# Linear attention and SwiGLU on one core: earlier start of the inputs, two more units turned by VectorE, weights' sums and two states moved

One Trainium2 chip (trn2), one core. The metric is the device time of one execution in microseconds (us). Most executions of one kernel agree within 0.3%.

## The reference

```python
# attention: B, H, S, D = 4, 8, 768, 48
for t in range(S):
    cur = einsum('bhd,bhe->bhde', u * k[t], v[t])
    y[t] = einsum('bhd,bhde->bhe', r[t], state + cur)
    state = w * state + einsum('bhd,bhe->bhde', k[t], v[t])
# x = y as (B*S, H*D) = (3072, 384); d_ff = 1536
g = x @ w_gate
out = (g * sigmoid(g) * (x @ w_val)) @ w_out
```

## The kernel before

A unit is 128 time steps of one batch (24 in all). For each, GpSimd scales k and r by powers of w, both are transposed, TensorE makes scores, outputs (y) and the state's update (u), and gates and projections of the feed-forward part fill TensorE between them. Units below `BLOCKS` are transposed by TensorE. Later ones are moved in 32-row blocks by 16 DMAs and then transposed by VectorE. Cuts are marked with `...`.

```python
for t in v_ld:
    dve.memset(t[:, :, D:64], 0.0)
dve.memset(hats[:, 0:6, :, D:64], 0.0)
dve.memset(wcol[:], 1.0)
for z in Z:
    pool.memset(z[:], 0.0)
for e in range(2):
    sp.dma_start(out=wcol[64 * e : 64 * e + D, :], in_=w...)
load(0)                         # k, r of unit 0, also by sp
...
make_identity(nc, ident[:])
warm(18)                        # dummy matmuls: TensorE's clock
...
dve.tensor_scalar(held[:], wcol[:], W_LOW, W_HIGH, ALU.max, ALU.min)
for l in range(7):              # L280: powers of w by doubling
    dve.tensor_mul(pw[:, :, P - 2 * n : P - n], pw[:, :, P - n : P], f)
...
own_product(0)                  # GpSimd: r * k, then * u

def rhat_of(i):
    return rhat[i % 2 if i < BLOCKS else i % 4 // 2]

def move_blocks(i):             # L356
    first, step = ((0, 1), (11, -1), (12, 1), (23, -1))[i % 4]
    for m in range(4):
        for q in range(4):
            sp.dma_start(out=..., in_=...)      # 32 x 256 values

def turn_blocks(i):             # L371
    for dst, src in ((kT[i % 2], blocks[0]), (turned[i], blocks[1])):
        dve.transpose(dst, src)

def weight_sum():               # L476, four times, 128 x 1152
    pool.tensor_sub(o, a, b)
...
turn(3)
dve.tensor_copy(w128[:].unsqueeze(2), pw[:, :, 0:1])
scores(2)
...
outputs(2)
load(4)
round_act()
feed(1)
outputs(3)
scale_k(3)
round_act()
round_pool()
scale(4)
load_v(4)
feed(1)
update(2)
update(3)
...
BLOCKS = 12
for s in range(4, N + 2):
    if 4 < s < N: own_sum(s)
    if s + 1 < N:
        scale(s + 1); own_product(s + 1); load_v(s + 1); load(s + 3)
    if s < BLOCKS: turn(s)
    gaps(s, 0)
    ... scores(s - 1) ...
    if BLOCKS <= s < N: turn_blocks(s)
    if BLOCKS <= s + 1 < N: move_blocks(s + 1)
    ...
```

Of the kernel before, what the change touches and what calls it, by code (L numbers as in the profile page):

```python
# [15 lines left out]
P = 128  # L16
# [6 lines left out]
def fast(  # L23
# [25 lines left out]
    B, H, S, D = r.shape  # L49
# [5 lines left out]
    N = B * NCH  # L55
    DM, DFF = moe_w_gate.shape
# [11 lines left out]
    dve, pool, act, pe, sp = nc.vector, nc.gpsimd, nc.scalar, nc.tensor, nc.sync  # L68


    wcol = cst.tile([P, HP], FP32, name="wcol")
# [3 lines left out]
    w128 = cst.tile([P, HP], FP32, name="w128")  # L75
# [11 lines left out]
    Z = [cst.tile([P, HP, D2], FP32, name=f"Z{b}") for b in range(B)]  # L87
# [12 lines left out]
    blocks = [hats[:, n].rearrange("p h x -> p (h x)") for n in (7, 6)]  # L100

    def rhat_of(i):
        return rhat[i % 2 if i < BLOCKS else i % 4 // 2]

    def raw(i):

# [125 lines left out]
    def own_sum(i):  # L232
        dus[i] = three.tile([P, H], FP32, name="du", tag="du")
        dve.tensor_reduce(dus[i][:], rks.pop(i), axis=AX.X, op=ALU.add)


    sg0 = two.tile([P, 1], FP32, name="sg0", tag="sg0")
    for t in v_ld:
        dve.memset(t[:, :, D:64], 0.0)
    dve.memset(hats[:, 0:6, :, D:64], 0.0)  # L240
    dve.memset(wcol[:], 1.0)
    for z in Z:
        pool.memset(z[:], 0.0)
    for e in range(2):
        sp.dma_start(out=wcol[64 * e : 64 * e + D, :], in_=w.rearrange("(a e) d -> e d a", e=2)[e])
    load(0)
    sp.dma_start(
        out=ub[:].rearrange("p h d -> p (h d)"),
# [10 lines left out]
    def warm(n):  # L259

        ps = ps_a.tile([P, HP, P], FP32, name="warm", tag="a")
        for _ in range(n):
            pe.matmul(ps[:, 0, :], ident[:], ident[:], start=True, stop=True)

    warm(18)

    pool.memset(mask[:], 1.0)
    pool.affine_select(
        out=mask[:], in_=mask[:], compare_op=ALU.is_gt, fill=0.0,
        base=0, pattern=[[1, P]], channel_multiplier=-1,  # L270
    )
    dve.tensor_scalar(held[:], wcol[:], W_LOW, W_HIGH, ALU.max, ALU.min)
    tables = two.tile([P, 2, HP, P + 32], FP32, name="tables", tag="hT")
    pw, pv = tables[:, 0, :, 0 : P + 1], tables[:, 1, :, 0:P]
# [2 lines left out]
    for l in range(7):  # L277
        n = 1 << l
# [19 lines left out]
    def scale_k(i):  # L298
        pool.tensor_mul(khat[i % 4][:, :, 0:D], raw(i)[0], kscale[:])  # L299
# [15 lines left out]
    def diagonal(i):  # L315

        du = dus.pop(i)
        on_act = HP if i < 4 else H
        small.extend(
            lambda h=h: act.activation(  # L320
                At[i % 2][:, h, :], ident[:], AF.Identity, scale=du[:, h : h + 1]
            )
            for h in range(on_act)
        )
        if on_act < H:
            n = H - on_act
            pool.tensor_mul(
                At[i % 2][:, on_act:H], ident[:].unsqueeze(1).to_broadcast([P, n, P]),
                du[:, on_act:H].unsqueeze(2).to_broadcast([P, n, P]),
            )  # L330
# [58 lines left out]
    def outputs(i):  # L389



        c, b = divmod(i, B)
        A, vl, z = At[i % 2], v_ld[i % 4], Z[b]
        rT = turned.pop(i)
        ps = ps_a.tile([P, CC, P], FP32, name="y_ps", tag="a")
        cols = [[] for _ in range(4)]
        for m in range(4 * CC):
            (cc, q), (a, s) = divmod(m, 4), divmod(m, 3)
            each = [(z[0:R2, a, 32 * s : 32 * s + 32], rT[0:R2, at(i, a), :])] if c > 0 else []  # L400
            if s < 2:
                each.append((vl[:, a, 32 * s : 32 * s + 32], A[:, 2 * a, :]))
            if s > 0:
                each.append((vl[:, a, 32 * s + 16 : 32 * s + 48], A[:, 2 * a + 1, :]))
            cols[q] += [(cc, x, n == 0, n == len(each) - 1) for n, x in enumerate(each)]
        for n in range(len(cols[0])):
            for q in range(4):
                cc, x, start, stop = cols[q][n]
                pe.matmul(  # L409
                    ps[32 * q : 32 * q + 32, cc, :], *x,  # L410
                    start=start, stop=stop, skip_group_check=True,
                )
        act.copy(xT[:, i % NX, :, :], ps[:])  # L413
# [57 lines left out]
    def weight_sum():  # L471

        n = len(summed)
        o = (wt[1][:], w12, wt[0][:], wt[2][:])[n]
        a, b = ((w22, w12), (w12, w11), (w22, w12), (w21, wt[0][:]))[n]
        pool.tensor_sub(o, a, b)  # L476
        summed.append(n)

    part_of = {}
# [18 lines left out]
    def project(g, n):  # L498

        h11, h12, h21, h22 = h_quarters(g)  # L500
        x = part_of.setdefault(g, {})
        if n == 0:
            one_bank = ps_f.tile([P, 2, 2 * P], FP32, name="o_f", tag="gv")[:, 0, 0:NH]
            if g % 2 == 0:
                x["a"] = ps_o.tile([P, 2 * P], FP32, name="o_a", tag="o")[:, 0:NH]
                x["b"] = one_bank
            else:
                x["a"] = one_bank
                x["b"] = ps_w.tile([P, 2 * P], FP32, name="o_b", tag="w_mag")[:, 0:NH]
            x["out"] = [two.tile([P, DM], FP32, name=n, tag=n) for n in ("o_sb1", "o_sb2")]  # L510
        lhs, rhs, acc = (
            (h11, w11, "a"), (h12, w21, "b"), (1, wt[0], "a"), (2, wt[1], "a"),
            (0, w12, "b"), (h22, wt[2], "a"), (3, w22, "b"),
        )[n]
        if isinstance(lhs, int):
            lhs = x["s"][lhs]
        ps = x[acc]
        for f in range(FH):
            pe.matmul(  # L519
                ps, lhs[:, f, :], rhs[:, f, :],  # L520
                start=(f == 0 and n in (0, 1, 4)), stop=(f == FH - 1), skip_group_check=True,
            )
        o1, o2 = x["out"]
        if n in (0, 2, 3):
            nm = {0: "p1", 2: "u2", 3: "u3"}[n]
            x[nm] = six.tile([P, 2 * P], FP32, name=nm, tag="part")[:, 0:NH]
            act.copy(x[nm], ps)
        elif n == 1:
            dve.tensor_add(o1[:, 0:NH], x["p1"], ps)
        elif n == 5:  # L530
            act.copy(o2[:, 0:NH], ps)
        elif n == 6:
            dve.tensor_add(o1[:, NH:DM], x["u2"], ps)  # L533
        if n in (3, 4):
            if "c22" in x:
                dve.tensor_add(o2[:, NH:DM], x["u3"], x["b"])
            x["c22"] = True
        if n >= 5:
            j = 6 - n
            c, b = divmod(2 * g + j, B)  # L540
            n0 = S * b + P * c
            act.dma_start(out=out[n0 : n0 + P, :], in_=x["out"][j][:])



# [130 lines left out]
    def feed(n, pops=1):  # L676
        for _ in range(n):
            ready = [k for k, (need, _) in enumerate(todo) if need <= done["pool"] + len(summed)]
            if ready:
                todo.pop(ready[0])[1]()  # L680
            for _ in range(min(pops, len(small))):
                small.popleft()()
# [32 lines left out]
                feed(1, 3)  # L715

    share = [0]
    BLOCKS = 12
    LATE = 12
    EARLY = {s: ("" if s < 7 else "R", "F", "R", "F", "RF") for s in range(5, 12)}  # L720
    EARLY[4] = ("R", "F", "", "F", "F")
# [6 lines left out]
    turn(0)  # L728
    natural_tables()
    own_sum(0)  # L730
    diagonal(0)
    flush()
    own_product(1)
# [38 lines left out]
    flush()  # L772
    own_product(3)
    turn(3)
    dve.tensor_copy(w128[:].unsqueeze(2), pw[:, :, 0:1])
    scores(2)
    update(0)
    update(1)
# [6 lines left out]
    load(4)  # L785
    round_act()
    feed(1)
    outputs(3)
    scale_k(3)
    round_act()  # L790
    round_pool()
    scale(4)
    load_v(4)
    feed(1)
    update(2)
    update(3)
    round_pool()
    own_product(4)
    load(5)
# [4 lines left out]
    for s in range(4, N + 2):  # L804
        if 4 < s < N:
            own_sum(s)
        if s + 1 < N:
            scale(s + 1)
            own_product(s + 1)
            load_v(s + 1)  # L810
            if s + 3 < N:
                load(s + 3)
        if s < BLOCKS:
            turn(s)
        gaps(s, 0)
        if 4 <= s - 1 < N:
            while small:
                small.popleft()()
            scores(s - 1)
            if s >= LATE:  # L820
                outputs(s - 2)
                update(s - 2)
            gaps(s, 1)
        if BLOCKS <= s < N:
            turn_blocks(s)
        if BLOCKS <= s + 1 < N:
            move_blocks(s + 1)
        gaps(s, 2)
        if s - 2 >= 4 and (s < LATE or s > N):
            outputs(s - 2)  # L830
            update(s - 2)
        if s >= 5 and s % 2:
            queue((s - 3) // 2)
        if s < N:
            diagonal(s)
        if s - 2 >= 4:
            gaps(s, 3)
        gaps(s, 4)
        if s == 12:

            dve.tensor_tensor(bad[:], held[:], wcol[:], ALU.not_equal)
            dve.tensor_reduce(badc[:], bad[:], axis=AX.X, op=ALU.add)
            dve.memset(ones[:], 1.0)
            n_ps = ps_a.tile([P, HP, P], FP32, name="n_ps", tag="a")
            pe.matmul(n_ps[0:1, 0, 0:1], badc[:], ones[:], start=True, stop=True)
            act.copy(outside, n_ps[0:1, 0, 0:1])
# [417 lines left out]
```

## Time and profile before

| | before |
|---|---|
| time, median of 3 | 625.08 us (624.19 to 625.53) |
| span in the profile | 623.3 us |
| TensorE busy | 98% |
| u of unit 4 begins | 59.33 us |
| u of unit 10 begins | 133.76 us |

TensorE bounds the kernel after about 58 us; the prediction shows the lines. I use two marks that can be read in every trace: the start of u (the state's update on TensorE) of unit 4 tells what the beginning is worth. The stretch from there to u of unit 10, 74.43 us here, tells what the stages around units 10 and 11 are worth. One place in that stretch matters below: the first pair's second and third projections. TensorE's timeline before (start, length, engine, line, operation, out<-in, shapes, count):

```profile
125.16 4.07 PE L519 MATMUL o_f<-wo,hT 128*128 128x192 f32 x24
```

The second and third projections run as one group of 24 matmuls, with no wait.

### The profile page before, as it was taken

What the parts mean: (1) busy time and instruction counts of PE and PEld (TensorE: products, weight loads), DVE (VectorE), ACT (ScalarE), POOL (GpSimd) and SP (SyncE); (2) the same over time, 40 slices, a digit from 0 to 9 for tenths busy, and PEclk for the clock granted to TensorE, in tenths of its full rate; (3) what the DMA queues carried; (4) which work ended last, traced back from release to release, by engine and by line L of the source; (5) the groups of instructions that cost most, each with busy time, mean ns of one, the idle gap of its engine ahead of it and who ended that gap; (6) DMA issues with size and microseconds to landing.
All of it is one profiled execution on the core that took longest, in us unless ns stands there. A gap on an engine that the chain in (4) does not pass through costs nothing.

```text
span 623.3 us, 13014 instructions
## 1 busy us (share of the span) xinstructions
PE 611.0 (98%) x5040; PEld 552.1 (89%) x5040; DVE 358.6 (58%) x751; ACT 238.9 (38%) x647; POOL 296.9 (48%) x350
## 2 busy tenths in 40 slices
PE   8799999999999999999999999999999999999996
PEld 7688888899888899888899888899988899988896
DVE  6888997373566574466575355574354463355460
ACT  3368785312444412344331335422243321233310
POOL 4789789935556315364452636341334211443110
PEclk9999999999999999999999999999999999999999
DMA  7989873233232213322223312221000000000001
GB/s 187 218 215 252 260 242 65 50 62 82 57 60 34 40 16 76 65 42 46 44 34 70 78 16 32 31 41 38 26 1 2 2 0 26 26 1 2 1 2 56
DMA packets 138008, 40.47 MB, mean 65 GB/s; under 512 B 128592, under 2 KB 131792, under 8 KB 137936
## 3 DMA queue, kind: packets, MB, share of 16 engines
q1 hardware_dynamic: 134480, 34.82, 26.4%
q10 hardware_dynamic: 3456, 4.72, 2.1%
q8 instruction: 42, 0.69, 0.5%
q14 instruction: 30, 0.25, 0.1%
HBM read 28.51 MB, written 4.72 MB: 53 GB/s over the span
## 4 chain that ended last, share of the span: by engine, by line
PE 90%; POOL 2%; DMA 1%; ACT 1%; DVE 1%; issue 0%; SPq 0%; ACTq 0%; POOLq 0%
PE c_b L625 25%; PE c_a L625 21%; PE o_f L519 13%; PE o_a L519 8%; PE gv L448 7%; PE o_b L519 6%; PE y_ps L409 5%; PE s_ps L379 3%; PE u_ps L424 1%; PE tp L341 1%; DMA r_ld<-in_r_dram 1%; POOL wg L216 1%; POOL wv L216 1%; POOL rk L228 0%; POOL hats L299 0%
## 5 line engine op out<-in xcount | busy, mean ns | idle before, releaser
L609 POOL TENSOR_TENSOR hT<-hT,u 128x256 f32<-128x256 f32 x60 | 47.0, 785 | 148.7 <-DVE hT L608 121.6
L632 ACT COPY u<-c_a 128x256 f32<-128x256 f32 x120 | 44.5, 371 | 85.8 <-PE c_a L625 83.3
L625 PE MATMUL c_a<-t,wv 128*128 128x256 f32 x240 | 72.1, 382 | 0.1
L625 PE MATMUL c_b<-xT,wg 128*128 128x256 f32 x240 | 71.7, 380 | 0.0
L605 ACT ACTIVATE sg<-hT 128x256 f32<-128x256 f32 x120 | 50.0, 416 | 52.5 <-DVE hT L634 33.8
L320 ACT ACTIVATE At<-ident,du 128x128 f32<-128x128 f32 x176 | 62.0, 398 | 16.0 <-DVE o_sb L533 7.2
L625 PE MATMUL c_b<-xT,s 128*128 128x256 f32 x240 | 61.7, 380 | 0.0
L639 DVE TENSOR_TENSOR u<-u,c_b 128x256 f32<-128x256 f32 x60 | 25.1, 419 | 60.5 <-PE c_b L625 55.4
L625 PEld LDWEIGHTS c_a<-t,wv 128*128 128x128 f32 x240 | 45.0, 190 | 6.8 <-ACT u L632 1.2
L625 PEld LDWEIGHTS c_b<-xT,s 128*128 128x128 f32 x240 | 45.3, 190 | 6.5
L625 PEld LDWEIGHTS c_b<-xT,wg 128*128 128x128 f32 x240 | 45.4, 190 | 5.9
L634 DVE TENSOR_TENSOR hT<-p,c_b 128x256 f32<-128x256 f32 x60 | 25.2, 420 | 41.7 <-PE c_b L625 39.1
L585 POOL TENSOR_TENSOR s<-wv,wg 128x256 f32<-128x256 f32 x24 | 17.6, 734 | 65.5 <-PE o_f L519 50.8
L384 DVE COPY_PREDICATED At<-mask,s_ps 128x512 f32<-128x512 int32 x48 | 33.0, 741 | 21.3 <-PE s_ps L379 12.4
L302 POOL TENSOR_TENSOR hats<-r_ld,rscale 128x384 f32<-128x384 f32 x20 | 20.8, 1040 | 35.3 <-DMA hats<-hats 25.2
L448 PE MATMUL gv<-xT,wg 128*128 128x256 f32 x144 | 36.7, 391 | 0.6 <-ACT xT L413 0.6
L637 DVE TENSOR_TENSOR hT<-hT,c_a 128x256 f32<-128x256 f32 x60 | 25.3, 421 | 19.5 <-PE c_a L625 18.3
L641 DVE TENSOR_TENSOR hT<-u,c_b 128x256 f32<-128x256 f32 x60 | 25.2, 421 | 19.4 <-PE c_b L625 19.2
L625 PE MATMUL c_b<-t,s 128*128 128x256 f32 x120 | 36.2, 383 | 0.0
L409 PE MATMUL y_ps<-At,v_ld 128*32 128x128 f32 x768 | 34.9, 273 | 1.3 <-DVE At L384 1.3
L625 PE MATMUL c_b<-xT,wv 128*128 128x256 f32 x120 | 35.9, 381 | 0.0
L625 PE MATMUL c_a<-t,s 128*128 128x256 f32 x120 | 35.8, 380 | 0.0
(135 smaller groups left out, 1384.3 us busy)
## 6 DMA issues: line engine op xcount, KB each, us to landing
hats<-hats SPq DMA_DIRECT2D x192, 32.0 KB, 2.0
w_bits<-in_moe_w_gate_dram SPq DMA_DIRECT2D x6, 768.0 KB, 6.4
v_ld<-in_v_dram SPq DMA_DIRECT2D x48, 96.0 KB, 3.3
w_bits<-in_moe_w_val_dram SPq DMA_DIRECT2D x6, 768.0 KB, 6.3
w_bits<-in_moe_w_out_dram SPq DMA_DIRECT2D x6, 768.0 KB, 6.7
out_dram<-o_sb ACTq DMA_DIRECT2D x24, 192.0 KB, 1.9
k_ld<-in_k_dram SPq DMA_DIRECT2D x20, 192.0 KB, 3.1
r_ld<-in_r_dram SPq DMA_DIRECT2D x20, 192.0 KB, 3.8
```

Of the source, the lines that this page charges most:

```text
L320: lambda h=h: act.activation(At[i % 2][:, h, :], ident[:], AF.Identity, scale=du[:, h : h + 1])
L384: dve.copy_predicated(At[i % 2][:].rearrange("p (a e) t -> p a e t", e=2)[:, :, e], mask[:].bitcast(INT32).unsqueeze(1).to_broadcast([P, H ...
L409: pe.matmul(ps[32 * q : 32 * q + 32, cc, :], *x, start=start, stop=stop, skip_group_check=True,)
L448: pe.matmul(gv[:, o, :].rearrange("p (i t) -> p i t", i=2), wt[:, c, P * f : P * (f + 1)], xT[:, 2 * g % NX : 2 * g % NX + 2, c, :], start ...
L519: pe.matmul(ps, lhs[:, f, :], rhs[:, f, :], start=(f == 0 and n in (0, 1, 4)), stop=(f == FH - 1), skip_group_check=True,)
L605: act.activation(x[what, f][:], h[j], AF.Sigmoid)
L609: pool.tensor_mul(h[1], h[1], x.pop(("u3", f))[:])
L625: pe.matmul(ps.rearrange("p (i t) -> p i t", i=2), lhs, rhs, start=first, stop=what not in ("p2", "p5", "p4", "p3"), skip_group_check=True,)
L632: act.copy(x[nm, f][:], ps)
L634: dve.tensor_add(h[0], x.pop(("p1", f))[:], ps)
L637: dve.tensor_mul(h[0], h[0], ps)
L641: dve.tensor_add(h[1], x.pop(("u2", f))[:], ps)
```

## The change

It has six parts. A: the memset of w's column comes first and w goes by ScalarE's queue, so that SyncE begins with k; 11 instead of 18 warm multiplies; the Z memsets behind the mask. B: units 10 and 11 turned by VectorE, and `turn` ahead of the scaling in the loop. C: the weights' sums on VectorE. D: the states of units 2 and 3 right behind y of unit 3. E: the w128 copy early. F: the last output stored in two halves. The intent is an earlier start and less work on TensorE.

```diff
-        return rhat[i % 2 if i < BLOCKS else i % 4 // 2]
+        return rhat[i % 2 if i < 8 else i % 4 // 2]
@@
+    dve.memset(wcol[:], 1.0)
     for t in v_ld:
         dve.memset(t[:, :, D:64], 0.0)
     dve.memset(hats[:, 0:6, :, D:64], 0.0)
-    dve.memset(wcol[:], 1.0)
-    for z in Z:
-        pool.memset(z[:], 0.0)
     for e in range(2):
-        sp.dma_start(out=wcol[64 * e : 64 * e + D, :], in_=w...)
+        act.dma_start(out=wcol[64 * e : 64 * e + D, :], in_=w...)
@@
-    warm(18)
+    warm(11)
     ... (mask) ...
+    for z in Z:
+        pool.memset(z[:], 0.0)
@@ weight_sum
-        pool.tensor_sub(o, a, b)
+        dve.tensor_sub(o, a, b)
@@ (part F, the last output in two halves: cut)
-    BLOCKS = 12
+    BLOCKS = 10
@@
     own_sum(0)
+    dve.tensor_copy(w128[:].unsqueeze(2), pw[:, :, 0:1])
@@
-    dve.tensor_copy(w128[:].unsqueeze(2), pw[:, :, 0:1])
     scores(2)
@@
+    scale_k(3)
     outputs(3)
-    scale_k(3)
+    update(2)
+    update(3)
     round_act()
     ...
     feed(1)
-    update(2)
-    update(3)
@@ loop over s
+        if s < BLOCKS:
+            turn(s)
         if s + 1 < N:
             scale(s + 1) ...
-        if s < BLOCKS:
-            turn(s)
```

More of the change, by code (lines that the diff above doesn't have):

```diff
@@ L240, in fast @@
     dve.memset(hats[:, 0:6, :, D:64], 0.0)
-    dve.memset(wcol[:], 1.0)
-    for z in Z:
-        pool.memset(z[:], 0.0)
     for e in range(2):
-        sp.dma_start(out=wcol[64 * e : 64 * e + D, :], in_=w.rearrange("(a e) d -> e d a", e=2)[e])
+        act.dma_start(out=wcol[64 * e : 64 * e + D, :], in_=w.rearrange("(a e) d -> e d a", e=2)[e])
     load(0)
@@ L537, in project, with store @@
             x["c22"] = True
-        if n >= 5:
-            j = 6 - n
+        def store(j, cols):
             c, b = divmod(2 * g + j, B)
             n0 = S * b + P * c
-            act.dma_start(out=out[n0 : n0 + P, :], in_=x["out"][j][:])
+            act.dma_start(out=out[n0 : n0 + P, cols], in_=x["out"][j][:, cols])
+        ends = g == N // 2 - 1
+        if n == 1 and ends:
+            store(0, slice(0, NH))
+        elif n >= 5:
+            store(6 - n, slice(NH if n == 6 and ends else 0, DM))
     PLACE = {
```

## The prediction

> **What bounds the kernel now.** I read the page's shares first, then the slices, the chain that ended last, the timelines of the first 60 us and of 100 to 136 us, and the groups by form.
>
> ```profile
> span 623.3 us, 13014 instructions
> PE 611.0 (98%) x5040; PEld 552.1 (89%) x5040; DVE 358.6 (58%) x751; ACT 238.9 (38%) x647; POOL 296.9 (48%) x350
> ...
> PE   8799999999999999999999999999999999999996
> ...
> POOL 4789789935556315364452636341334211443110
> ...
> PE 90%; POOL 2%; DMA 1%; ACT 1%; DVE 1%; issue 0%; SPq 0%; ACTq 0%; POOLq 0%
> ```
>
> TensorE bounds the kernel. Only the first two slices (0 to 31 us) and the last are not full, and GpSimd (POOL) is full in the third to eighth slices. In the chain in order of time everything from 57.8 us to the end is TensorE; before that it runs through POOL:
>
> ```profile
> 52.90 1.80 POOL wv L216
> 54.73 0.93 ACT w_low L179
> 57.76 1.75 PE y_ps L409 x56
> 59.85 5.38 PE gv L448 x24
> ```
>
> So a gain before 57.8 us counts if it moves that POOL chain; after it, only TensorE work removed or a new TensorE wait counts. The start, from the timeline:
>
> ```profile
> 0.80 1.48 POOL L243 MEMSET Z<- 128x384 f32 x4 [0.29 <-POOLq L1248]
> 2.08 0.88 SPq L245 DMA_DIRECT2D wcol<-in_w_dram  x2
> 2.84 6.83 PE L263 MATMUL warm<-ident 128*128 128x128 f32 x36 [2.84 <-POOL ident masks.py:199]
> 3.00 0.45 SPq L115 DMA_DIRECT2D hats<-in_k_dram  x1
> 4.53 0.17 DVE L272 TENSOR_SCALAR held<-wcol 128x4 f32<-128x4 f32 x1 [2.49 <-DMA wcol<-in_w_dram]
> 7.52 0.99 POOL L228 TENSOR_TENSOR rk<-hats 128x384 f32<-128x384 f32 x1 [4.22 <-DMA hats<-in_r_dram]
> 9.39 0.91 PEld L341 LDWEIGHTS tp<-ident,hats 128*128 128x128 f32 x8
> 26.61 0.96 DVE L775 COPY w<-tables 128x4 f32<-128x4 f32 x1
> ```
>
> k and r are there by 7.5 us, but the first real transpose starts at 9.39: the warm matmuls hold TensorE until then, and the tables made from w end at 9.06 (7.63 + 1.43, same view).
>
> **What the Trainium skill says.** (1) "TensorE: Matmul & The Clock Gate", "What's actually happening": the array runs at half clock until a free-running window of about 3.4 us was busy. The trace agrees: the warm weight loads take 334 ns until about 7.3 us and 192 ns from 8.5. (2) "SBUF — State Buffer", "Who interferes with whom": a VectorE op of the two-port kind or with two SBUF inputs and a GpSimd op block each other whole. The 128x4 copy of L775 took 0.96 us beside a GpSimd multiply of 1.01 us that had begun at 26.54. (3) "DMA: Bandwidth & Descriptors", "Anatomy of one DMA": about 2 us fixed per DMA; the page here has 2.0 us for the hats<-hats moves. It reads them as fixed latency; issue is what I must add to it below.
>
> **The change, part by part.**
>
> *Start.* SyncE no longer waits for the memset of wcol nor issues w: k goes out at about 0.8 instead of 3.00, and the whole input stream behind it moves up by 2.2 us (the first eight slices are DMA-heavy, so it stays shifted). w goes out by ScalarE's queue at about 1.0 instead of 2.08 and lands at about 3.5 to 4.0 instead of 4.5: tables end at 8.0 to 8.6. ident is ready 1.4 us earlier, as the Z memsets move behind; 11 warm multiplies at two passes of about 0.213 us (cold start-to-start) run 1.4 to 6.1. Then the transposes run as soon as k and r land (about 5.3) and VectorE's first table multiply starts at about 8.1 to 8.6 instead of 10.14. That is 1.5 to 2.2, say 2.0 us, up to 20 us. Seven fewer warm multiplies alone are worth nothing beyond this, as they lie beside the wait for the tables.
>
> *w128.* VectorE has no listed wait from 20.57 to 30.8 us, so the 0.96 us there come off: gain 2.9 at 31 us. At its new place VectorE had 0.67 us idle.
>
> *States of 2 and 3.* Their four VectorE multiplies (1.47 us at 39.54) now come ahead of the second chunk's rounding, which ended at 38.34. POOL wanted that chunk at 39.30, so about 1.47 - 0.96 = 0.5 us are lost on the POOL chain. TensorE fills a 0.60 us wait with the u products, but is held by POOL there anyway. Gain at 57.8 us: 2.9 - 0.5 = 2.4 us.
>
> *Units 10 and 11.* 16 transposes leave TensorE. By the chain eight take 0.87 us, with the step to the scores 0.97: 1.94 us on a full TensorE. Four ScalarE copies (0.58 each) go, four VectorE transposes (0.71 + 0.67 per unit) come, and 32 moves of 32 KB. Those are the dear part:
>
> ```profile
> 118.82 0.37 SPq L115 DMA_DIRECT2D k_ld<-in_k_dram  x1
> 119.87 10.90 SPq L356 DMA_DIRECT2D hats<-hats  x16
> 132.57 1.02 POOL L302 TENSOR_TENSOR hats<-r_ld,rscale 128x384 f32<-128x384 f32 x1 [7.98 <-DMA hats<-hats]
> 123.83 0.42 DVE L455 TENSOR_TENSOR sg<-sg,gv 128x256 f32<-128x256 f32 x1 [2.41 <-ACT sg L454]
> ```
>
> Sixteen issues take 10.9 us, and GpSimd's next rhat waits 1.8 us past them. A stage here lasts only 12.15 us (tp at 101.67 and 113.81). In the times of the kernel before: the k load for unit 12 is issued at 94.14, so unit 10's moves run 95.2 to 106.0; rhat of 11, which overwrites their source, starts at 107.8; then the k product to 109.9, the load of unit 13 to 111.0, unit 11's moves to 121.9, landed about 123.6. VectorE meets unit 11's transposes at about 118.3 in its order, so it sits about 5 us, then has 1.38 (transposes), 0.74 (Z) and 0.85 (the last gate's two multiplies) before it: done at about 126.6. Those multiplies free the PSUM bank for the second projection, which TensorE began at 125.16 and would now reach at 125.16 - 1.94 = 123.2. So it waits 3.4 us, and the pair nets 126.6 - 125.1 = 1.5 us worse instead of 1.94 better. Unit 12 and later have stages twice as long and are not held.
>
> *Weights' sums.* Four GpSimd ops of 2.65 us become VectorE ops of about 1.3 (0.95 for 768 columns, times 1152/768, minus a fixed part). GpSimd has room for them, VectorE too, beside the wait above; GpSimd needs the relief, as it now waits at rhat of 11. Nothing on TensorE's path.
>
> *End.* The last store carries half the bytes; landing is mostly fixed (1.9 us): 0.2 us.
>
> Sum: -2.4 + 1.5 - 0.2 = -1.1, about 624.0; without the wait at unit 11: -2.4 - 1.94 - 0.2 = -4.5, about 620.5.
>
> **Rivals.** (a) The moves hide. For it: VectorE does only 58% overall, and if issue is faster with less traffic, or unit 10's moves begin earlier, each us saved in one set of moves comes off twice. Against: both sets measured 10.9 and 10.5 us. It gives 620.5. (b) My main account, 624.0: the transfer's latency takes the place of the transposes removed. (c) The start gives less: w from ScalarE shares the rings with k and r and lands no earlier, or TensorE goes cold between 6 and 8 us; gain 1 instead of 2.4, hence 622 to 625.4 with (a) or (b). (d) The start gives more: POOL keeps all of the 2.9 and the half us is not lost; 620.0 with (a), 623.5 with (b).
>
> **Range and chances.** I put 0.55 on the wait at unit 11 costing most of what I worked out, and 0.45 on it being small. The mean of 624.0 and 620.5 with these weights is 622.4; I say 622.5, with 619.5 to 624.9 for 8 in 10. The 2% border is at 612.6 and 637.6: no sum of the parts comes near either, so within 2% has 0.97.
>
> **What would show it.** Right: first transposes at about 6 to 7 us; VectorE's first table multiply before 8.7; the w128 copy away from 26 us; TensorE's steady stretch begins about 2.4 us earlier, as does y of unit 4 (57.76 before); VectorE idle for 3 to 5 us at unit 11's kT transposes, released by hats<-hats, and TensorE idle up to 3.4 us before the second projection's o_f. If neither idle stretch is there, (a) is right. Wrong altogether: a TensorE wait after 140 us, new waits of GpSimd at the w sums, or a first TensorE wait that grew for lack of k and r.

## The result, and the profile after

The changed kernel takes 628.4 us, median of 6 (627.33 to 631.55), against 625.12 us (624.19 to 625.53) of the kernel before. The ratio is 1.0064, 95% interval 1.0037 to 1.009. Ratios are the mean time of one kernel's fast runs over that of the other's of the same rounds, so not quite the ratio of the medians quoted. The result is within 2%, but it lies outside my range and on the other side of the kernel before. All runs count as fast, yet they spread over 4 us, with mean granted clocks of 0.99 to 1.0.

The page of the profile after, span and busy times:

```profile
span 627.2 us, 12991 instructions
PE 608.4 (97%) x5010; PEld 547.2 (87%) x5010; DVE 368.2 (59%) x759; ACT 236.9 (38%) x643; POOL 290.2 (46%) x346
```

TensorE does 2.6 us less work (611.0 before), and the span is 3.9 us longer: all of the loss, and more, is waiting. The two marks are 59.50 us for u of unit 4 (59.33 before) and 78.12 us for the stretch to unit 10 (74.43 before). From there to the end nothing more is lost: 3.86 us of the 3.93 us by which the last projection ends later are there at unit 10.

**The start.** Timeline after, all engines:

```profile
5.31 0.17 DVE L272 TENSOR_SCALAR held<-wcol 128x4 f32<-128x4 f32 x1 [3.25 <-DMA wcol<-in_w_dram]
5.54 1.01 POOL L228 TENSOR_TENSOR rk<-hats 128x384 f32<-128x384 f32 x1 [2.23 <-DMA hats<-in_r_dram]
5.72 3.22 DVE L280 TENSOR_TENSOR tables<-tables 128x4 f32<-128x4 f32 x7
8.99 0.66 PE L308 MATMUL t_ps<-ident,tables 128*128 128x128 f32 x4 [2.08 <-DVE tables L280]
10.38 0.68 DVE L343 TENSOR_TENSOR kT<-tp,tables 128x512 f32<-128x512 f32 x1
```

k and r land 2 us earlier (GpSimd's product begins at 5.54, 7.52 before), but w lands later, 5.31 against 4.53. The list of DMA issues shows it; its last column is the median time from issue to landing, of the kernel before and then of the one after:

```profile
wcol<-in_w_dram SPq DMA_DIRECT2D x2, 0.8 KB, 1.9
```

```profile
wcol<-in_w_dram ACTq DMA_DIRECT2D x2, 0.8 KB, 3.3
```

On ScalarE's queue w travels beside k and r, and takes 3.3 us instead of 1.9; its own queue did not bring it earlier here. Then the seven doublings took 3.22 us, against 1.85 before, because GpSimd's products now lie beside them. Part of that is won back: before, the last multiply of the tables (L284, at 7.63) lay beside GpSimd's product and took 1.43 us, after only 0.69. So the tables end 5.15 us after w, 4.53 before, and with the later w they end at 10.46 instead of 9.06. The first table multiply starts at 10.38, not at 8.1 to 8.6. That is only 0.24 us later than before (10.14), because before it had waited for TensorE's transposes, which began at 9.39. TensorE, which had run out of warm multiplies, stands idle for 2.08 us. GpSimd's first addition of low parts (L197), where its long chain begins, starts at 18.00 us, against 18.01 before: of the 2.0 us that the start was to give up to 20 us, nothing is there.

**The states.** VectorE and GpSimd after:

```profile
35.64 1.45 DVE L434 TENSOR_TENSOR Z<-u_ps,w 48x192 f32<-48x192 f32 x4
37.13 0.56 DVE L188 TENSOR_SCALAR wv<-w_mag 128x384 int32<-128x384 int32 x1
39.48 1.83 POOL L216 TENSOR_TENSOR wv<-wv,w_low 128x768 int32<-128x768 int32 x1 [0.64 <-DVE wv L189]
```

The Z multiplies of units 2 and 3 stand between the roundings of two chunks, and GpSimd, whose chain sets the pace up to unit 4, waits 0.64 us for the second.

**Units 10 and 11.** The queue of SyncE, GpSimd, VectorE and TensorE after:

```profile
97.10 11.90 SPq L356 DMA_DIRECT2D hats<-hats  x16
111.40 1.01 POOL L302 TENSOR_TENSOR hats<-r_ld,rscale 128x384 f32<-128x384 f32 x1 [5.67 <-DMA v_ld<-in_v_dram]
114.48 11.23 SPq L356 DMA_DIRECT2D hats<-hats  x16
127.11 0.71 DVE L371 STREAM_TRANSPOSE kT<-hats 128x512 f32<-128x512 f32 x1 [4.34 <-DMA hats<-hats]
```

```profile
130.09 2.19 PE L519 MATMUL o_f<-wo,hT 128*128 128x192 f32 x12 [2.27 <-DVE hT L456]
132.84 1.38 PE L519 MATMUL o_a<-wt,hs 128*128 128x192 f32 x7 [0.56 <-DVE hs L493]
```

The chain of the prediction is there: moves of 10, scaled r of 11, moves of 11, VectorE waiting 4.34 us, TensorE waiting 2.27 us. But it is the third projection that waits, not the second. In this one trace two more things came on top, which the later trace of the same kernel (run 16) does not show: a chunk of weights landed late (the stretch up to unit 7 was 0.98 us longer), and a gate waited 1.10 us at 116 us.

### The profile page after: what moved, and what is told of

Same layout as the page of the kernel before. It is cut to its first block, busy times and chain, and to the rows that moved or that the text cites. A ratio compares the mean times of both kernels' runs of the same rounds, so it can differ in the third digit from the quotient of the medians.

```text
span 627.2 us, 12991 instructions
## 1 busy us (share of the span) xinstructions
PE 608.4 (97%) x5010; PEld 547.2 (87%) x5010; DVE 368.2 (59%) x759; ACT 236.9 (38%) x643; POOL 290.2 (46%) x346
## 4 chain that ended last, share of the span: by engine, by line
PE 78%; DVE 4%; POOL 4%; SPq 3%; DMA 2%; ACT 2%; issue 1%; ACTq 0%; POOLq 0%; DVEq 0%
PE c_b L630 25%; PE c_a L630 21%; PE o_f L519 12%; PE o_a L519 7%; PE o_b L519 6%; PE y_ps L409 4%; SPq L356 3%; PE s_ps L379 2%; DMA w_bits<-in_moe_w_out_dram 1%; ACT At L320 1%; POOL rk L228 1%; DMA r_ld<-in_r_dram 1%; POOL wo L216 1%; POOL wg L216 1%; ACT w_low L179 1%
```

## The experiments

Sixteen kernels ran, one of them the changed kernel again. The kernel before was timed in each job: median 625.10 (runs 1 to 4), 625.02 (5 to 8), 625.47 (9 to 12), 625.69 (13 to 16). "Stretch" is from u of unit 4 to u of unit 10 in the profiled execution.

| run | time, median (range) | ratio, 95% interval | u of unit 4 | stretch |
|---|---|---|---|---|
| before | | | 59.33 | 74.43 |
| changed | 628.4 (627.33-631.55) | 1.0064, 1.0037-1.0090 | 59.50 | 78.12 |
| 1 not units | 627.47 (625.67-628.90) | 1.0046, 1.0033-1.0059 | 59.53 | 74.43 |
| 2 units only | 625.98 (625.00-628.01) | 1.0021, 1.0005-1.0036 | 58.94 | 74.25 |
| 3 start only | 625.49 (624.54-626.77) | 1.0005, 0.9992-1.0018 | 59.80 | 74.43 |
| 4 w128, states | 625.89 (625.64-626.46) | 1.0014, 1.0001-1.0027 | 59.89 | 74.43 |
| 5 sums on GpSimd | 628.37 (627.47-629.32) | 1.0055, 1.0041-1.0068 | 59.63 | 76.50 |
| 6 start, 18 warms | 624.54 (624.02-625.57) | 0.9997, 0.9983-1.0010 | 58.28 | 74.51 |
| 7 GpSimd held | 624.98 (623.99-625.39) | 0.9999, 0.9985-1.0012 | 58.12 | 74.43 |
| 8 w first | 623.67 (623.32-624.52) | 0.9981, 0.9967-0.9994 | 57.82 | 74.43 |
| 9 filled, 16 | 627.53 (627.11-629.49) | 1.0034, 1.0021-1.0047 | 61.55 | 76.26 |
| 10 unit 11 only | 625.19 (624.52-626.97) | 0.9996, 0.9982-1.0009 | 59.24 | 73.55 |
| 11 alternate buffers | 626.38 (625.07-626.73) | 1.0011, 0.9998-1.0024 | 58.76 | 74.62 |
| 12 filled, sums on GpSimd | 627.72 (627.26-629.27) | 1.0043, 1.0030-1.0056 | 59.75 | 76.25 |
| 13 states on start | 625.36 (624.97-626.88) | 1.0000, 0.9988-1.0012 | 59.53 | 74.43 |
| 14 w first, unit 11 | 623.82 (623.13-624.44) | 0.9976, 0.9963-0.9989 | 58.28 | 73.55 |
| 15 filled, 9 | 627.72 (627.29-628.60) | 1.0036, 1.0023-1.0049 | 61.47 | 75.12 |
| 16 changed again | 628.44 (626.41-629.91) | 1.0039, 1.0023-1.0055 | 61.54 | 76.83 |

The marks are single traces; where they and the times differ, I say so.

**1. All parts but B.**

```diff
 # the changed kernel, with BLOCKS = 12, turn(s) behind the scaling, rhat_of as before
```

> All of the change except that units 10 and 11 stay with TensorE. Theory W (the chain of 32 moves at units 10 and 11 cost TensorE about 4.4 us between 102 and 133 us, set against 1.94 us saved): about 2 to 2.5 us under the changed kernel in the same job, that is 625.5 to 626.5, with no TensorE wait longer than 0.6 us between 100 and 140 us and no VectorE wait for hats<-hats there. Rival S (the loss comes from the start and the order of rounding, the moves net to nothing): same time as the changed kernel, 628.

Measured 627.47 us, with one execution at 625.67 (clock 1.0) and two near 628.8 (clock 0.992). The stretch is that of the kernel before, so B accounts for the whole lengthening of the stretch. The median lies between the two expectations (625.5 to 626.5, and 628), so neither theory had the time right. The parts outside B gain nothing at unit 4, and the slow executions are those with a low clock.

**2. B alone on the kernel before.**

```diff
-    BLOCKS = 12
+    BLOCKS = 10
 # turn(s) ahead of scale(s + 1); rhat_of with i < 8
```

> The kernel before with only the units 10 and 11 moved to VectorE (with the order of turning and scaling that it needs), weights' sums still on GpSimd. Theory W: slower than before by 1.5 to 4 us, a VectorE wait of 3 to 5 us at unit 11's kT transposes released by hats<-hats; GpSimd's sums (4 x 2.65 us) may delay unit 11's scaling further. Rival S: within 0.5 us of before or up to 1.9 us faster.

```profile
122.86 0.71 DVE L371 STREAM_TRANSPOSE kT<-hats 128x512 f32<-128x512 f32 x1 [5.09 <-DMA hats<-hats]
```

```profile
125.84 2.19 PE L519 MATMUL o_f<-wo,hT 128*128 128x192 f32 x12 [0.70 <-POOL wt L476]
128.42 2.19 PE L519 MATMUL o_a<-wt,hs 128*128 128x192 f32 x12 [0.39 <-DVE hs L493]
```

The first fence is VectorE, the second TensorE. VectorE waits 5.09 us at 122.86, as predicted ("about 5 us"), and TensorE waits 0.70 and 0.39 us at the third and fourth projections. The stretch is 0.18 us shorter, not 1.5 us longer: the bank that the late gate frees is used by the third projection, one projection (1.95 us from start to start) later than I had it. Where the 1.94 us go can be read: up to u of unit 9 the stretch is 1.74 us shorter (58.99 us, 60.73 before), and the last stage, from there to u of unit 10, is 1.56 us longer (15.26, 13.70 before). In time this kernel is none the less slower than the kernel before by 0.2% (1.0005 to 1.0036), 0.9 us in the medians, which is neither theory W's 1.5 to 4 us nor rival S's 0.5 us at most. Half of the executions were nevertheless at 626.75 to 628.01 us, at clocks of 0.995 to 0.998, and the other half at 625.0 to 625.2.

**3. A alone.**

```diff
 # kernel before, with w by act, wcol memset first, Z memsets behind the mask, warm(11)
```

> The kernel before with only the new start: w by ScalarE's queue, SyncE begins with k, 11 warm multiplies, memsets reordered. From the trace of the changed kernel (first transposes at 5.8 us, but tables multiplied only from 10.38 against 10.14) I expect no gain: 624.6 to 625.6, the w column landing at about 5.3 us against 4.5, and the seven doubling multiplies of the tables taking about 3.2 us against 1.85 because GpSimd's rk products run beside them. The prediction's theory would have it 2 us faster.

Windows of this trace (stretch, length, busy time and count of PE, PEld, DVE, ACT, POOL, then the granted clock, the DMA share, GB/s):

```profile
8.00:12.00 4.00, 1.93 (x10) 1.73 (x11) 3.83 (x10) 0.63 (x2) 0.00 (x0) 0.78 1.08 334
12.00:16.00 4.00, 4.00 (x43) 3.79 (x42) 2.02 (x4) 2.81 (x7) 3.02 (x3) 0.80 1.38 222
```

TensorE is busy for only 1.93 of 4 us in 8 to 12 us, and its clock falls to 0.78 and 0.80. u of unit 4 comes at 59.80, later than before. Three executions had a clock of 0.995 and took 626.2 to 626.8 us; three had 0.998 to 1.0 and took 624.5 to 624.8. So the shorter warm-up is no mere saving.

**4. D and E alone.**

```diff
 # kernel before, with the w128 copy behind own_sum(0), and scale_k(3), outputs(3), update(2), update(3)
```

> The kernel before with only the two small moves: the w128 copy early, the states of 2 and 3 right behind y of 3. If the 0.96 us of the copy come off VectorE's stretch and the states' 1.45 us ahead of the second rounding take them back, as the trace of the changed kernel suggests (wv rounding at 37.13 against 36.14, GpSimd's wv add at 39.48 against 39.30): within 0.4 us of before. If the prediction's sizes were right: 0.4 to 0.5 us faster.

u of unit 4 came 0.56 us later than before, and the time was 625.89 us. My prediction gave these two parts 0.4 us of gain (0.96 minus 0.5). The w128 copy took 0.16 us at its new place, but VectorE then waited 0.49 us for scores at 26.96, so only half of the 0.96 us arrived: VectorE's next masked copy is 0.53 us ahead of the kernel before (26.96, 27.49), and the one after that only 0.15 us (31.84, 31.99). The states then took 0.7 us. The expectation (within 0.4 us of before) failed: the median is 0.79 us above.

What takes away the second part of the gain shows in all traces. With the copy at its new place VectorE waits 1.57 to 1.58 us for the masked copy of unit 3 (at 31 to 33.5 us; nine traces: the changed kernel, runs 1, 4, 5, 9, 12, 14, 15 and 16). With the copy at the old place it waits 1.22 us in all nine others. So the early copy itself comes with 0.36 us lost at that step; why, no run shows.

**5. The sums back on GpSimd.**

```diff
-        dve.tensor_sub(o, a, b)
+        pool.tensor_sub(o, a, b)
```

> The changed kernel with the four weights' sums back on GpSimd. Theory P (the sums on VectorE cost: 1.6 to 2.1 us each instead of the 1.3 I had estimated, GpSimd's rk products beside them twice as long, both ahead of unit 11's moves and of the last gates): 1.5 to 2.5 us under the changed kernel, 626 to 627, and VectorE at unit 11's kT transposes by about 123 instead of 127.1 us. Rival: the sums are neutral and 628 stays.

628.37 us, ratio 1.0055: not told apart from the changed kernel, which was not in this job (1.0064 in its own, 1.0039 in run 16). TensorE's wait at the third projection was 1.90 us here, and behind it the clock fell to 0.81 (125 to 130 us) and 0.85 (130 to 135 us): the twelve matmuls took 3.83 us instead of 2.11. The sums are not what costs, though on VectorE they took 1.64 to 2.13 us each, not the 1.3 us I had worked out.

**6. A with the 18 warm multiplies kept.**

```diff
-    warm(11)
+    warm(18)
```

> The new start alone, but with all 18 warm multiplies. Theory C (the idle stretch of TensorE between the first transposes and the tables lets its clock fall in some executions, which is why the start alone ran at 624.5 to 624.8 with a mean clock of 0.998 and at 626.2 to 626.8 with 0.995): every execution at 624.5 to 625.5 and no mean clock of 0.995 or less. Rival D (the two levels come from the transfers): two levels again.

Three executions took 624.02 to 624.54 us at a clock of 0.999, two 625.52 and 625.57 at 0.996. The group of run 3 at 0.995 and over 626 us is gone, as theory C has it; a smaller second group remains. u of unit 4 is at 58.28: this start is worth 1.05 us there, not 2.4. The time is not told apart from the kernel before (0.9983 to 1.0010).

**7. GpSimd held until the tables are done.**

```diff
+    junk = cst.tile([P, 1], FP32, name="junk")
+    pool.tensor_copy(junk[:], pv[:, 0, 0:1])     # waits for the tables
     own_product(0)
```

> As the run before it, and GpSimd held until the tables are made by a one-column copy from them. Theory P (two VectorE inputs in SBUF against a GpSimd op): the seven doublings take 1.85 us again instead of 3.2, the tables are done about 1.3 us earlier (9.8 instead of 10.4), and as rk of unit 0 then starts late, at most 0.5 us come off the total. Rival: the doublings stay at 3.2 us because of something else.

```profile
5.63 1.85 DVE L280 TENSOR_TENSOR tables<-tables 128x4 f32<-128x4 f32 x7
```

With GpSimd out of the way the doublings take 1.85 us again, as before the change. That shows the cause of the 3.22 us. It gains little at unit 4 (58.12), as GpSimd's product then comes late.

**8. w by SyncE, ahead of k.**

```diff
-        act.dma_start(out=wcol...
+        sp.dma_start(out=wcol...
```

> As the run before it, but w goes out by SyncE ahead of k again, right after the early memset of wcol. If k and r ahead of w on the shared rings are what made w land at 5.3 instead of 4.5 us: w lands at 3.3 to 3.6, the tables are done by 8.2, the first table multiply at 8.2 to 8.9 instead of 10.14, and the whole is 0.5 to 1.5 us under the kernel before. If the landing of w does not follow the order of issue: no change against the run before it.

```profile
3.41 0.17 DVE L272 TENSOR_SCALAR held<-wcol 128x4 f32<-128x4 f32 x1 [1.35 <-DMA wcol<-in_w_dram]
```

This kernel also keeps run 7's holding of GpSimd. w lands at 3.41, and the tables are done at 7.19 instead of 10.46. 623.67 us, faster than the kernel before (ratio at most 0.9994), and u of unit 4 is 1.51 us earlier. So w behind k and r was the wrong thing to change: w is 0.8 KB and the tables wait for it. The edit moves w back to SyncE's queue and ahead of k at once, so the runs do not tell which of the two did it.

**9. The changed kernel with TensorE's idle times filled.**

```diff
-    warm(11)
+    warm(18)
@@ ahead of the third projection of the first pair
+            if g == 0 and (j, p) == (0, 1):
+                warm(16)
```

> The changed kernel with 18 warm multiplies at the start again and 16 more dummy multiplies (about 1.7 us at full clock) put on TensorE just ahead of the third projection of the first pair, where it stood idle for 2.27 us. My theory: part of the loss is the clock that falls behind such an idle stretch (0.80 behind the start with 11 warms, 0.81 behind the projection's wait in an earlier trace). Then no slice of the trace but the first shows a clock under 1.0, the executions lie within 1 us of each other at clocks of 0.996 or more, and the time is 626 to 627 instead of 628.4. Rival, waits alone: the executions still spread over 627 to 631 us with clocks of 0.993 and the median stays near 628.

The dummies took about 3.5 us, not 1.7, and so overshot the wait by about 2 us (the last gate ended at 129.16, the projection began at 131.15). At the projections the clock stays at 1.00. But the profiled execution (629.49 us) shows a fall at another place:

```profile
25.00:26.00 1.00, 0.32 (x9) 0.13 (x5) 1.00 (x3) 0.57 (x2) 1.00 (x2) 1.00 1.08 348
...
29.00:30.00 1.00, 1.00 (x10) 0.90 (x8) 0.95 (x3) 0.00 (x0) 0.00 (x0) 0.50 0.76 283
...
33.00:34.00 1.00, 1.00 (x4) 0.82 (x3) 0.90 (x2) 1.00 (x3) 0.16 (x1) 0.50 0.07 16
```

From 28 to 34.5 us TensorE runs at half clock, though no wait of it in the 8 us before was longer than 0.69 us; u of unit 4 comes at 61.55. My expectation (all executions within 1 us, clocks of 0.996 or more) failed.

**10. Only unit 11 turned by VectorE.**

```diff
-    BLOCKS = 12
+    BLOCKS = 11
 # on the kernel before, with the rest of part B
```

> The kernel before with only unit 11 turned by VectorE. Eight transposes leave TensorE (0.97 us with the step to the scores), and only one set of moves comes ahead of unit 12's. If the loss of the pair is that two sets of about 11.3 us follow each other in stages of 12, then unit 11's moves start near 96 to 107 us, VectorE's kT transpose of unit 11 waits for no DMA for more than 0.5 us, u of unit 10 begins at about 132.8 instead of 133.76, and the time is 624.0 to 624.4. Rival, that the place of the turn ahead of the scaling or VectorE's transposes themselves cost it: u of unit 10 at 133.5 or later, the time 625 or more.

```profile
124.19 4.06 PE L519 MATMUL o_f<-wo,hT 128*128 128x192 f32 x24
```

The second and third projections are again one group of 24, without a wait, and the stretch is 0.88 us shorter, close to the 0.97 us of eight transposes. VectorE still waited 2.76 us for the moves, more than the 0.5 us I expected, but TensorE did not feel it. The time, 625.19 us, is not told apart from 625.47 in the same job, and missed the 624.0 to 624.4 us expected.

**11. B alone, with the scaled r of neighbouring units in alternate buffers.**

```diff
-    khat = planes (0, 2, 3, 5)
+    khat = planes (0, 3, 2, 5)
-        return rhat[i % 2 if i < 8 else i % 4 // 2]
+        return rhat[i % 2]
-        ((0, 1), (11, -1), (12, 1), (23, -1))[i % 4]
+        ((0, 1), (12, 1), (11, -1), (23, -1))[i % 4]
```

> The kernel before with units 10 and 11 turned by VectorE, and with the scaled r of neighbouring units in alternate buffers, so that unit 11's need not wait until unit 10's moves have read theirs. Theory: the chain moves of 10, scaled r of 11, product rk of 11, load of 13, moves of 11 is what makes VectorE late. Then GpSimd's scaled r of unit 11 comes at about 103 instead of 107.17, unit 11's moves start at 107.5 to 108.5 instead of 110.24, VectorE's wait at kT of unit 11 falls from 5.09 to 2 to 3 us, TensorE's waits of 0.70 and 0.39 at the projections go, u of unit 10 begins at 131.8 to 132.3 (133.19 with the units alone, 133.76 before), and the time is 623.2 to 624.0. Rival, the 11.3 us of issue of each set alone: the wait stays over 4 us and the time is as of the units alone, 625 to 626.

The queue of SyncE, TensorE, and GpSimd:

```profile
108.89 11.90 SPq L356 DMA_DIRECT2D hats<-hats  x16
```

```profile
128.60 2.19 PE L519 MATMUL o_a<-wt,hs 128*128 128x192 f32 x12 [1.24 <-DVE hs L493]
```

```profile
127.60 1.71 POOL L228 TENSOR_TENSOR rk<-r_ld,k_ld 128x384 f32<-128x384 f32 x1
```

GpSimd's scaled r of unit 11 did come at 102.75, 4.4 us earlier than in run 2. But unit 11's moves began only 1.35 us earlier (110.24 there), since the queue had unit 10's moves (11.78 us) and four loads to issue first, and VectorE still waited 4.61 us. So the rival holds: the time to issue two sets of moves is the bound, not the buffer. And GpSimd's scaling and product now lay beside VectorE's sums of h, which took up to 1.75 us instead of 0.95, and TensorE waited 1.24 us for them.

**12. As run 9, with the sums on GpSimd.**

```diff
 # run 9, with pool.tensor_sub in weight_sum
```

> As the filled version of the changed kernel, but with the weights' sums left on GpSimd. If the sums on VectorE cost (they took 1.6 to 2.1 us each and slowed GpSimd's products beside them to 2.0 us, and the changed kernel's gates waited 1.10 us at 116 us), this one is 1.0 to 1.5 us faster than the filled version: 625 to 626. Rival, that they are off the path as predicted: both within 0.5 us.

627.72 against 627.53 us, stretches of 76.25 and 76.26: no difference, the rival of my expectation. But both have the overshoot of the 16 dummies in them, about 2 us, which would hide a smaller one. The last gate of the pair ended 67.23 us after u of unit 4 here and 67.61 in run 9; without dummies, in runs 5 and 16, 67.95 and 68.16. So part C costs at most 0.2 to 0.4 us at that place.

**13. D on the start of run 6.**

```diff
+    scale_k(3)
     outputs(3)
-    scale_k(3)
+    update(2)
+    update(3)
     ...
-    update(2)
-    update(3)
```

> The start of the change with 18 warm multiplies (624.54 us in an earlier job, u of unit 4 at 58.28) plus the states of units 2 and 3 moved up, and nothing else. Theory: the four Z multiplies (1.47 us) now stand on VectorE between the two roundings of weights, GpSimd's add of the second comes 1.0 to 1.5 us later, u of unit 4 begins at 59.3 to 59.8, and the time is 625.5 to 626.0: this part alone eats what the start gives. Rival, the half us of my prediction: u of unit 4 at 58.8, time 625.0. Rival, off the path: 624.5.

GpSimd's addition to the second chunk, in run 6 and then in run 13:

```profile
38.25 1.83 POOL L216 TENSOR_TENSOR wv<-wv,w_low 128x768 int32<-128x768 int32 x1
```

```profile
39.09 1.82 POOL L216 TENSOR_TENSOR wv<-wv,w_low 128x768 int32<-128x768 int32 x1 [0.66 <-DVE wv L189]
```

A wait of 0.66 us appears, and u of unit 4 is 1.25 us later (59.53 against 58.28). Of this the states account for about 0.7 us. GpSimd's addition is 0.84 us later, of which 0.14 us were there before the states' turn, and in run 6 the chunk had been ready 0.95 us before GpSimd wanted it. Another 0.4 us or so goes with a chunk of weights that landed late in this trace (ScalarE waited 2.54 us for it at 54.49). In time, 1.0000 against 0.9997 in another job, the difference is not resolved.

**14. The useful parts together: w first, 18 warms, GpSimd held, unit 11 alone, early w128 copy.**

```diff
 # run 8, with BLOCKS = 11 and the rest of part B, and the w128 copy behind own_sum(0)
```

> A candidate that should beat both: w ahead of k on SyncE, 18 warm multiplies, GpSimd's first product held until the tables are made (623.67 us in an earlier job, against 625.02 of the kernel before), with unit 11 alone turned by VectorE and the early w128 copy. If the gains add: -1.35, -0.97 and about -0.2, so 622.3 to 622.9, u of unit 4 near 57.7 and u of unit 10 near 131.1. If unit 11 falls into the DMA wait: 623.7.

623.82 us against 625.69 in its job, ratio 0.9976 (0.9963 to 0.9989): faster than both kernels. The stretch shows the 0.88 us of unit 11, but u of unit 4 came at 58.28, 0.46 us later than in run 8, so the gains did not add in full. Of the 0.46 us, 0.36 is the longer wait that the early copy brings (see run 4): VectorE's masked copy of unit 3 begins at 30.98, in run 8 at 30.52. The time is not told apart from run 8, and missed the 622.3 to 622.9 us expected.

**15. The changed kernel with 18 warms and 9 dummies.**

```diff
+            if g == 0 and (j, p) == (0, 1):
+                warm(9)
```

> The changed kernel with 18 warm multiplies and 9 dummies (18 passes of 0.11 us, 1.98 us; the 16 dummies of the earlier run took 3.52 us and overshot the 2.27 us wait). If clock falls behind TensorE's idle stretches make up part of the loss, the time is 626.0 to 626.8, and at least 1 us below the changed kernel of the same job. If only the waits count: within 0.5 us of the changed kernel.

The stretch is 75.12 us, 1.7 us shorter than in run 16, with the clock at 1.00 throughout it; what is left over the kernel before is 0.69 us, of which about 0.6 is the dummies' overshoot (they ended at 129.50, the last gate at 128.91). The median is 627.72 us, 0.7 us below run 16 and not the 1 us I required; the two are not told apart (1.0023 to 1.0049, 1.0023 to 1.0055). And the profiled execution again had half clock from 28 to 34.5 us. So filling one hole did not give one clean level.

**16. The changed kernel again, without an edit.**

> The changed kernel itself in the same job, for comparison: 627.3 to 631.5, median about 628.4; the theory of the clock says that the executions at 0.996 or more are the fast ones.

```profile
12.00:16.00 4.00, 4.00 (x33) 3.67 (x34) 1.99 (x5) 2.69 (x7) 3.01 (x3) 0.61 1.37 221
130.00:135.00 5.00, 5.00 (x21) 4.64 (x22) 4.42 (x6) 0.00 (x0) 0.65 (x1) 0.66 0.41 60
```

```profile
9.40 0.66 PE L308 MATMUL t_ps<-ident,tables 128*128 128x128 f32 x4 [2.73 <-DVE tables L280]
129.85 2.87 PE L519 MATMUL o_f<-wo,hT 128*128 128x192 f32 x12 [1.93 <-DVE hT L456]
```

This is the clearest view of the clock's part of the loss. In the profiled execution (629.91 us, clock 0.993) TensorE waited 2.73 us for the tables, and the clock fell to 0.61 in the windows behind it (clock column, 12 to 16 us). It waited 1.93 us for the last gate, and the clock fell to 0.66 behind that. Worked out from the two windows, 4 x 0.39 + 5 x 0.34 = 3.3 us at most. The execution with clock 0.999 took 626.41 us, 0.7 us above the kernel before; the four at 0.993 took 627.28 to 629.91. So the clock alone does not order them: my expectation that the fast executions are those at 0.996 or more failed at 627.28. And the first profiled execution of this kernel (628.98 us) had clock 1.00 in every window: its whole loss is waits.

## Why the prediction was wrong, point by point

- **The start, 2.0 us of the -2.4 us at 57.8 us: failed, and this is the larger error.** The mark at unit 4 moved by +0.17 instead of -2.4, or by +2.2 in the execution with the clock fall (61.54). The steps that failed are the landing of w and the time from w to the tables. *w lands at 3.5 to 4.0*: it landed at 5.31, beside k and r. I had named this in rival (c) and given it 1.4 us. *Tables about 4.5 us after w, as before* (4.53): they ended 5.15 us after it, because k and r, being earlier, brought GpSimd's products beside the doublings, which took 3.22 us instead of 1.85 (run 7 shows it); the last multiply, now free of them, gave 0.7 us back. I had cited the very rule for the w128 copy and not applied it here. *Transposes at about 5.3*: near (5.87), but they are not what the next step waits for: the first table multiply waits for the tables, and came at 10.38 instead of 8.1 to 8.6.
- **The sum up to unit 4, as measured.** At 25 us VectorE is 0.14 us ahead of the kernel before, where 2.0 us was predicted. From there to GpSimd's addition of the second chunk the terms, as measured, are 0.14 + 0.75 (copy) - 0.36 (the longer wait behind the early copy) - 0.69 (states) = -0.16 us; the trace has it 0.18 us late (39.48, 39.30). One reading of mine at the start was also off: the warm weight loads take 334 ns until about 7.9 us, not 7.3.
- **w128, -0.96 us: too large.** The copy took 0.16 us where it was put, and VectorE's next masked copy is 0.89 us ahead in the changed kernel (0.14 of it the start's). But VectorE then waits 0.36 us longer for the one after it (run 4), so about half arrives. And in run 6 the old copy took only 0.27 us once the start had shifted it away from GpSimd's multiply: on a start that works, most of this gain is already in it, so the sum counted it twice.
- **States, +0.5 us: the mechanism right, the size too small.** The term was 1.47 - 0.96 = 0.5. The slack of 0.96 us is there (0.95 in run 6), but the states delay GpSimd's addition by about 0.7 us in all three places: the changed kernel, run 4 and run 13. GpSimd's waits of 0.64 and 0.66 us show it.
- **Units 10 and 11, +1.5 us: the chain right, the place wrong.** VectorE's wait of about 5 us and its release by the moves came as told. The late bank belongs to the third projection, which gives TensorE 1.95 us more. In run 2 the net is -0.18 instead of +1.5. In the changed kernel at full clock about 0.69 us remain (run 15, with the dummies' overshoot in it). Unit 11's moves begin later there than in run 2 (in run 5, all parts but C, 52.3 us behind the mark of unit 4, against 51.3); why is not shown.
- **Weights' sums, nothing on TensorE's path: right within what the runs can tell: at most 0.2 to 0.4 us at the last gate of the pair (runs 9 and 12, 5 and 16).** The duration was wrong (1.64 to 2.13 us, not 1.3), and one trace had a gate waiting 1.10 us at 116 us; no other showed it.
- **End, -0.2 us: nothing to be seen.** From the end of the last projection to the end of the span it is 5.29 us, against 5.32 before. No run had part F alone.
- **What the sum lacked: the clock.** Every term took TensorE's idle time as idle time alone. Behind the waits of 2.73 and 1.93 us in run 16 the clock fell to 0.61 and 0.66, worth up to 1.6 and 1.7 us in those two windows. Of the twelve timed executions of the changed kernel ten have a mean clock of 0.997 or less (of the kernel before in the last job, three of eleven), and the traces show such falls behind idle stretches. Rival (c) has half a sentence on a TensorE that goes cold, and no number.

Put together: the fastest execution of the changed kernel in run 16 is 0.7 us above the kernel before, which the waits explain (0.17 at unit 4 and 0.69 in the stretch make 0.9). For the other 2 us of the median, the clock is the likeliest cause, but not shown to be the whole of it. That the clock falls is shown (runs 3, 5, 9, 15 and 16); its share is argued from the clocks of the executions. Against it: waits alone made 628.98 us at clock 1.00, an execution of run 16 took 627.28 us at 0.993, and run 15, where the fall at the projections was gone, reached only 627.72 us. What decides whether an execution has such a fall stays open, as do the executions of run 15 at clock 0.999 (627.29 and 627.72 us), which are slower than run 16's at 0.999.

## What to carry to other kernels

On an engine that sets the end, count an idle stretch of about 2 to 3 us twice: once as itself, and once as what the clock may lose behind it (here between nothing and about 1.7 us). Dummy multiplies while the inputs are late helped at the start (run 6 against run 3). Put the small transfer that everything waits for first, ahead of the large ones, and when inputs are brought forward look at which engine's work is brought beside which. Two gains that both come from moving the same wait are one gain. And moving a small operation can change what a later one waits for (0.36 us behind the early copy).

## What the Trainium skill lacked or had wrong

- "TensorE: Matmul & The Clock Gate", "What's actually happening" and "HAM oscillation — how this bites in real kernels": the page ties the return to half clock to an idle window of about 3.4 us. Here the clock fell behind idle stretches of 2.73, 1.93 and 1.90 us (runs 16 and 5), and to exactly 0.50 for 6.5 us with no wait over 0.69 us in the 8 us before it (runs 9 and 15, among small, partly filled matmuls). A wait of 2.27 us at the same place left it at 1.00 in another execution. Of short gaps the page has, for one kernel and without a length, that brief idles between groups of matmuls can make the clock oscillate ("A second HAM failure mode: psum-queue depth-cycling"); it gives no gap as short as 1.9 us. Its remark that the window is free-running would fit the chance in it; no run tests that.
- "DMA: Bandwidth & Descriptors", "Issuing engines are not separate DMA queues": that DMAs of all issuing engines run on the same 16 engines and interleave fits w's 3.3 us beside k and r. But it calls the time to initiate a DMA usually small relative to the DMA itself. For the moves of 32 KB within SBUF the issue took 0.65 to 0.76 us each (16 in 10.40 to 12.10 us over all runs), and this issue is what bounded VectorE in run 11.
- "SBUF — State Buffer", "Who interferes with whom": agrees, but gives no size for chains of tiny operations. Here seven multiplies on 128x4 to 128x256 values took 3.22 us instead of 1.85 beside two GpSimd products of 1.0 us.
